# A Fourier-filter and squared-ReLU block on one core: reordered GpSimd queue, inverse stages by row group, stage-2 runs of four, and a first chunk normalised in the drain

## The chip, the cores and the metric

One core of a Trainium2 chip runs the kernel. The metric is the device time of one launch in microseconds (us). Before the change three runs gave 183.88, 184.01 and 184.28 us; the median is 184.01. The profile is of one execution, and the span of its instructions is 182.5 us.

## The reference, cut to what matters

The input is one sequence of 2048 rows of 512 bf16 values. Two residual blocks follow each other. The first normalises each row and filters it in the two-dimensional Fourier domain; the second normalises again and runs a dense layer pair with a squared ReLU.

```python
def _layernorm(x, axis=-1, eps=1e-5):
    m = jnp.mean(x, axis=axis, keepdims=True)
    v = jnp.var(x, axis=axis, keepdims=True)
    return (x - m) / jnp.sqrt(v + eps)

def _A_ref(x, w_r, w_i):                      # w_r, w_i: [2048, 257]
    X = rfft2(x.astype(float32))              # over both axes
    return irfft2(X * (w_r + 1j * w_i), s=(S, D)).astype(bfloat16)

def _B_ref(x, w1, b1, w2, b2):                # w1: [512, 1792], w2: [1792, 512]
    h = x @ w1 + b1
    r = where(h > 0, h, 0)
    return (r * r) @ w2 + b2

h  = A_x + _A_ref(_layernorm(A_x), A_w_r, A_w_i)
h2 = h   + _B_ref(_layernorm(h), B_w1, B_b1, B_w2, B_b2)
```

## The kernel before

Row number 16·p + g of the input lies in partition p, row group g (16 groups of 128 rows). Both transforms are done by matmuls with sine and cosine tables that the kernel makes itself: stage 1 (`s1`) contracts over p, stage 2 (`s2`) over the 512 columns, stage 3 (`s3`) over what is left of the rows; then comes the product with W on VectorE; stage 4 (`s4`), stage 5 (`d5` or `s5`) and stage 6 (`d6` or `s6`) go back. The rows then go through the two dense layers in five chunks of 2, 3, 4, 4 and 3 row groups (`CHUNKS`). Every task is given to a planner with an estimated duration; the planner fixes the order of each engine's instructions, and each engine keeps that order.

The normalisation of the first block is folded into the stage-1 table: `KR` is the table times the reciprocal root of a row's variance, and GpSimd computes that root. The same GpSimd queue halves one column of W (the last one) once W has been loaded.

```python
BATCH = ((0, 4), (4, 8), (8, 12), (12, 14), (14, 16))
for bi, (a, b) in enumerate(BATCH):
    ...
    pool(..., lambda a=a, b=b: gp.tensor_tensor(rs1[:, a:b], rs1[:, a:b], mhalf[:, 0:b - a], ALU.pow), z - 1,
         reads=[("va", bi), "mhalf"], writes=[("rs", bi)])                        # the roots
    for g in range(a, b):
        dve(0.22, lambda g=g: ve.tensor_scalar(flat(KR[:, g]), flat(KF[:]), rs1[:, g:g + 1], WSC, ALU.mult, ALU.mult), ...,
            reads=[("rs", bi), "KF"], writes=[("KR", g)], shared=True)
...
for k, (a, b) in (("n", (0, 9)), ("r", (9, 16))):
    for i in range(2):
        pool(0.15, lambda ...: gp.tensor_scalar(W[i][:, a:b, L - 1:L], W[i][:, a:b, L - 1:L], 0.5, None, ALU.mult), 300.0,
             reads=[("W" + k, i)], writes=[("Wh" + k, i)])                        # half of the last column
```

Stages 2 and 3 run in eight steps `pr`. The stage-2 result leaves PSUM for a bf16 tile U in which the two parts `e` of the result alternate element by element, and stage 3 reads U in straight runs. Steps 4 to 7 (`BY_PE`) take their last butterfly on TensorE (twelve matmuls), the others on VectorE (four matmuls and two additions, `bf`).

```python
def eu(...):
    U = buf(fwd, ("U", pr), "U", [P, 2, 512], BF16, 3)
    eng(U[:].rearrange("p q (c e) -> p q e c", e=2)[:, a:b], pu[:].rearrange("p (q e c) -> p q e c", e=2, c=256))
def s3(pr=pr):
    ...
    mm(a, lhsT=C, rhs=U[:, 0, :], start=True, stop=False)
    mm(b, lhsT=C, rhs=U[:, 1, :], start=True, stop=False)
    mm(a, lhsT=N, rhs=U[:, 1, :], start=False, stop=True)
    mm(b, lhsT=S_, rhs=U[:, 0, :], start=False, stop=True)
```

The stage-4 result of each step is copied to T2, whose dimensions are [quarter l, group g, q, s]. For the last step (7) four copies are made: groups 0 and 1 of each half of the quarters, then groups 2 to 15 of each half.

```python
T2 = persist.tile([P, 4, G, 16, 8], BF16, name="T2")
def et(eng=sc.copy, pr=pr, h=0, n=4, a=0, b=G):
    dst = T2[:, 2 * h:2 * h + n, :, 2 * pr:2 * pr + 2, :].rearrange("p l g q s -> p l q g s")
    ...
    eng(dst[:, :, :, a:b], src[:, 2 * h:2 * h + n, :, a:b])
```

Groups 0 and 1 (chunk 0) are not normalised before the first dense layer. A transposed copy `yt` of x minus its mean plus the filter's result is accumulated on TensorE (the x part early, in `yt_pre`, with the mean as a two-row matmul), copied to `UT0`, and multiplied by W1 as it is. Since ReLU of a positive multiple is that multiple of the ReLU, the standard deviation is put on the bias instead: each of the 14 first-layer results gets a further matmul with two contraction rows, b1 times the standard deviation, and the output is divided by the variance at the end.

```python
for f in range(NF):                                       # NF = 14
    def up(...):
        for d in range(ND):
            mm(p[:, 0:P * n], lhsT=W1[:, d, bass.ts(f, P)], rhs=(T["UT", c] if c else UT0)[:, d, 0:P * n],
               start=(d == 0), stop=(d == ND - 1 and c > 0))
    if c == 0:
        add("PE", 0.216 * n, up, reads=[("UT", c), ("FW", 0)], writes=[("pa", f)], ...)
        add("PE", 0.11, lambda f=f: mm(T["ph", 0, f][:, 0:256], lhsT=b1row[:, bass.ts(f, P)], rhs=flat(srow[:]),
                                       start=False, stop=True),
            reads=["srow", ("FW", 4)], ...)
```

Of the kernel before, what the change touches and what calls it, by code (L numbers as in the profile page):

```python
# [9 lines left out]
ALU = mybir.AluOpType  # L10
# [139 lines left out]
def kernel(  # L150
# [37 lines left out]
    T2 = persist.tile([P, 4, G, 16, 8], BF16, name="T2")  # L188
# [7 lines left out]
    sd0 = persist.tile([P, 2], FP32, name="sd0")  # L196
    mhl = persist.tile([P, 2, 2], BF16, name="mhl")
    shl = persist.tile([P, 2, 2], BF16, name="shl")
    mrow = persist.tile([2, 2, P], BF16, name="mrow")
    srow = persist.tile([2, 2, P], BF16, name="srow")  # L200
    b1row = persist.tile([2, F], BF16, name="b1row")
    one2 = persist.tile([2, P], BF16, name="one2")
# [3 lines left out]
    UT0 = persist.tile([P, ND, 2 * P], BF16, name="UT0")  # L206
# [10 lines left out]
    CN = fwd.tile([P, 4, P], BF16, name="CN")  # L217
# [29 lines left out]
    plan = Plan({"mm": 2, "sg": 4, "U": 3, "AB": 3, "X": 2, "mA": 2, "mB": 2, "Z": 2, "M": 2, "st": 4, "EO": 2,  # L247
# [33 lines left out]
    for c, (a, b) in enumerate(CH):  # L281
# [7 lines left out]
    add("SP", 0.5, lambda: sy.dma_start(b1row[:], B_b1.unsqueeze(0).to_broadcast([2, F])), writes=[("FW", 4)], prio=35,  # L289
        order=[("Wr", 1)], lag=6.0)  # L290
    for i in range(2):
        add("SP", 1.6, lambda i=i: sy.dma_start(wx[i][:].rearrange("k j l -> j k l"),
                                                wv[i].rearrange("k j l -> j k l")[9:16, ::-1, 1:L + 1]),
            writes=[("wx", i)], prio=6 + i, at=1.0, lag=6.0)
        add("SP", 1.2, lambda i=i: sy.dma_start(W[i][:, 0:9, :], wv[i][:, 0:9, 1:L + 1]), writes=[("Wn", i)],  # L295
            prio=20 + i, at=1.0, lag=7.0)
        add("SP", 0.8, lambda i=i: sy.dma_start(W[i][:, 9:16, :], wx[i][:]), reads=[("wx", i)], writes=[("Wr", i)],
            prio=22 + i, lag=5.0)
# [86 lines left out]
    for bi, (a, b) in enumerate(BATCH):  # L385
# [22 lines left out]
        for g in range(a, b):  # L408
            dve(0.22, lambda g=g: ve.tensor_scalar(flat(KR[:, g]), flat(KF[:]), rs1[:, g:g + 1], WSC, ALU.mult, ALU.mult), z - 5,  # L409
                reads=[("rs", bi), "KF"], writes=[("KR", g)], shared=True)  # L410
    for g in range(G):
# [15 lines left out]
        def e1(eng, g0, key=key):  # L427
            n = 2 if g0 < 10 else 1
            dst = Bt[:].rearrange("p e q (g s) -> p e g q s", s=8)[:, :, g0:g0 + n]
            COPY[eng](dst, T[key][:].rearrange("p (i e q s) -> p e i q s", e=4, q=16, s=8))  # L430
        if not big:
            add(("ACT", "DVE"), (0.59, 0.67), lambda e, g=g, e1=e1: e1(e, g), reads=[key], writes=["Bt"], prio=56 + g)
        elif g % 2:
            act(0.93, lambda g=g, e1=e1: e1("ACT", g - 1), 10 + g, reads=[key], writes=["Bt"])
# [12 lines left out]
    PE0, PE1, PES = 4, 8, 1  # L447
# [4 lines left out]
    for lt in range(4):  # L452
# [7 lines left out]
    dve(0.1, lambda: ve.memset(one2[:], 1.0), 190.0, writes=["one2"])  # L460
    dve(0.13, lambda: ve.tensor_copy(mhl[:, :, 0], nm1[:, 0:2]), 200.0, reads=["nm1"], writes=["mh"], shared=True)
    dve(0.13, lambda: ve.tensor_tensor(mhl[:, :, 1], nm1[:, 0:2], mhl[:, :, 0], ALU.subtract), 200.0, reads=["mh"],
        writes=["mhl"], shared=True)

    dve(0.15, lambda: ve.tensor_copy(b1f[:], b1b[:]), 200.0, reads=[("FW", 2)], writes=["b1f"], shared=True)

    def mid_tasks():
        act(1.07, lambda: sin_of(flat(GI[:]), lo(flat(fiI[:]))), 125.0, reads=["fiI"], writes=["GI"])
        act(1.4, lambda: sc.activation(junk[:, 0:1], eps[:], ACT.Sqrt), 0.0, reads=["GI", "eps", ("p4", SQ)], writes=["sqrt"])
        def mr():  # L470
            p = sg_tile(("mr", 0))
            for g in range(2):
                mm(p[0:2, P * g:P * g + P], lhsT=mhl[:, g, :], rhs=ident[:], start=True, stop=True)
        add("PE", 0.12, mr, reads=["mhl", "ident"], writes=[("mr", 0)], prio=110.0, alloc=("sg", ("mr", 0)))
        act(0.25, lambda: sc.copy(flat(mrow[:]), T["mr", 0][0:2, 0:2 * P]), 110.0, reads=[("mr", 0)], writes=["mrow"])

        def yt_pre(g):
            y = sg_tile(("yt", g))
            mm(y[:], lhsT=one2[:], rhs=mrow[:, g].unsqueeze(1).to_broadcast([2, 4, P]), start=True, stop=False)
            for d in range(ND):  # L480
                mm(y[:, P * d:P * d + P], lhsT=xs[:, g, P * d:P * d + P], rhs=ident[:], start=False, stop=False)
        for g in range(2):
            add("PE", 0.44, lambda g=g: yt_pre(g), reads=["mrow", "one2", "ident"], writes=[("yt", g, 0)], prio=145.0 + g,
                uses=[("yt", g)], alloc=("sg", ("yt", g)))

    for k, (a, b) in (("n", (0, 9)), ("r", (9, 16))):
        for i in range(2):
            pool(0.15, lambda i=i, a=a, b=b: gp.tensor_scalar(W[i][:, a:b, L - 1:L], W[i][:, a:b, L - 1:L], 0.5, None,
                                                              ALU.mult), 300.0,
                 reads=[("W" + k, i)], writes=[("Wh" + k, i)])  # L490
    gfv = GF[:].rearrange("p t r (e j) -> p t r e j", e=2)
    Z0 = 80

    for pr, first in ((0, 1), (1, 1), *((p, 0) for p in range(8))):
# [12 lines left out]
        if first or pr > 1:  # L507
# [12 lines left out]
            def eu(pr=pr, a=0, b=2, eng=sc.copy, new=True):  # L520
                U = buf(fwd, ("U", pr), "U", [P, 2, 512], BF16, 3) if new else T["U", pr]
                pu = T[("p2", pr, a) if pr < 2 else ("p2", pr)]
                eng(U[:].rearrange("p q (c e) -> p q e c", e=2)[:, a:b], pu[:].rearrange("p (q e c) -> p q e c", e=2, c=256))
            if pr < 2:
                for q in range(2):
                    add(("ACT", "DVE"), (0.66, 0.7), lambda e, pr=pr, eu=eu, q=q: eu(pr, q, q + 1, COPY[e], q == 0),
                        reads=[("p2", pr, q)], order=[("U", pr, 0)] * q, writes=[("U", pr), ("U", pr, q)],
                        alloc=None if q else ("U", ("U", pr)), prio=z + 2)
            else:
                act(1.17, eu, z + 2, reads=[("p2", pr)], writes=[("U", pr)], alloc=("U", ("U", pr)))  # L530

        ab = ("X", pr) if pr == 0 or pr in BY_PE else ("AB", pr)
        if pr == 0 and first:
            def s3z(u):
# [3 lines left out]
                mm(o[:], lhsT=C, rhs=U[:, u, :], start=True, stop=False)  # L538
                mm(o[:, 0:256], lhsT=S_, rhs=U[:, u, 256:512], start=False, stop=False)
                mm(o[:, 256:512], lhsT=N, rhs=U[:, u, 0:256], start=False, stop=True)  # L540

            def ea0(u, eng):
                X = buf(fwd, ("X", 0), "AB", [P, 2, 2, 256], BF16, 3) if u == 0 else T["X", 0]
                eng(flat(X[:, u]), T["p3", 0, u][:])
            for u in range(2):
                add("PE", 0.46, lambda u=u, s3z=s3z: s3z(u), reads=[("U", 0, u), "EF0", "EF1", "EF2"], order=[("p3", 0, j) for j in range(u)],
                    writes=[("p3", 0, u)], prio=z + 1, alloc=("sg", ("p3", 0, u)))
                add(("ACT", "DVE"), (0.59, 0.67), lambda e, u=u, ea0=ea0: ea0(u, COPY[e]), prio=z + 1, reads=[("p3", 0, u)],
                    order=[("X", 0, 0)] * u, writes=[("X", 0), ("X", 0, u)], alloc=None if u else ("AB", ("X", 0)))
        elif pr > 0 and not first:  # L550
            def s3(pr=pr):
# [4 lines left out]
                if pr in BY_PE:  # L556
                    Cn = CN[:, BY_PE.index(pr), :]
                    r, i = slice(0, 256), slice(256, 512)
                    mm(a, lhsT=C, rhs=U[:, 0, :], start=True, stop=False)
                    mm(b, lhsT=C, rhs=U[:, 0, :], start=True, stop=False)  # L560
                    mm(a[:, r], lhsT=C, rhs=U[:, 1, i], start=False, stop=False)
                    mm(b[:, i], lhsT=C, rhs=U[:, 1, r], start=False, stop=False)
                    mm(a[:, i], lhsT=Cn, rhs=U[:, 1, r], start=False, stop=False)
                    mm(b[:, r], lhsT=Cn, rhs=U[:, 1, i], start=False, stop=False)
                    mm(a[:, r], lhsT=S_, rhs=U[:, 0, i], start=False, stop=False)
                    mm(b[:, i], lhsT=S_, rhs=U[:, 0, r], start=False, stop=False)
                    mm(a[:, i], lhsT=N, rhs=U[:, 0, r], start=False, stop=False)
                    mm(b[:, r], lhsT=N, rhs=U[:, 0, i], start=False, stop=False)
                    mm(a, lhsT=N, rhs=U[:, 1, :], start=False, stop=True)
                    mm(b, lhsT=N, rhs=U[:, 1, :], start=False, stop=True)  # L570
                else:
                    mm(a, lhsT=C, rhs=U[:, 0, :], start=True, stop=False)
                    mm(b, lhsT=C, rhs=U[:, 1, :], start=True, stop=False)
                    mm(a, lhsT=N, rhs=U[:, 1, :], start=False, stop=True)
                    mm(b, lhsT=S_, rhs=U[:, 0, :], start=False, stop=True)
# [23 lines left out]
        def prod(pr=pr, i=0):  # L599
            m = buf(fwd, (("mA", "mB")[i], pr), ("mA", "mB")[i], [P, 2, 2, 256], BF16, 2)  # L600
            sel = slice(0, 9, 8) if pr == 0 else slice(pr, 17 - pr, 16 - 2 * pr)
            ve.tensor_tensor(m[:], T["X", pr][:], W[i][:, sel].unsqueeze(2).to_broadcast([P, 2, 2, 256]), ALU.mult)
        for i in range(2):
# [46 lines left out]
        def et(eng=sc.copy, pr=pr, h=0, n=4, a=0, b=G):  # L650
            dst = T2[:, 2 * h:2 * h + n, :, 2 * pr:2 * pr + 2, :].rearrange("p l g q s -> p l q g s")
            src = T["p4", pr][:].rearrange("p (l q g s) -> p l q g s", l=4, q=2, g=G)
            eng(dst[:, :, :, a:b], src[:, 2 * h:2 * h + n, :, a:b])  # L653
        if pr < 7:
            act(0.93, et, z + 3, reads=[("p4", pr)], writes=["T2", "T2a"])
        else:
            for h in range(2):
                add(("ACT", "DVE"), (0.25, 0.22), lambda e, h=h, et=et: et(COPY[e], 7, h, 2, 0, 2), prio=z, reads=[("p4", 7)],
                    writes=["T2a", ("T2a", h)])
                add(("ACT", "DVE"), (0.53, 0.6), lambda e, h=h, et=et: et(COPY[e], 7, h, 2, 2, 16), prio=z + 90,  # L660
                    reads=[("p4", 7)], order=["T2a"], writes=["T2", ("T2r", h)])

# [29 lines left out]
    for g in range(2):  # L692
        for e in (1, 0):
            ptag = "pp" if g else "po"

            def d5(g=g, e=e, ptag=ptag):
                p = bank(("pd", g, e), ptag, 3 if g else 2)
                for r in range(2):
                    mm(p[:, 0:256], lhsT=flat(T2[:, 2 * r + e, g]), rhs=GI[:, 2 * r + e, :], start=(r == 0), stop=(r == 1))
# [7 lines left out]

            def yt(g=g, e=e):
# [251 lines left out]
```

## Time and profile before

| what | value |
|---|---|
| median time | 184.01 us (183.88 to 184.28) |
| span of the profiled execution | 182.5 us |
| PE, matmul, busy | 164.4 us (90%), 1096 instructions |
| DVE busy | 123.6 us (68%) |
| ACT busy | 110.3 us (60%) |
| POOL busy | 15.3 us (8%) |
| chain that ended last | PE 75%, DVE 9%, DMA 7% |

PE is TensorE, DVE VectorE, ACT ScalarE, POOL GpSimd, and SPq the queue that issues the transfers. The profile's line of 40 slices gives the busy tenths of each engine in slices of 4.6 us. The chain of work that ended last starts at the last instruction and goes back, at each step, to what released it. Its pieces are printed in order of time as start, duration and what ran. A timeline row has the start, the duration and the instruction with its count; square brackets give the idle time of the engine before it and what ended it. [...] a group of matmuls is better measured from the start of one to the start of the next.

### The profile page before, as it was taken

The page shows a single profiled execution, that of the slowest core. Times are in us where ns is not written, and L with a number is a line of the kernel's source. Part 1 is how long each engine was busy: PE and PEld are TensorE (multiplying, and loading weights), DVE is VectorE, ACT ScalarE, POOL GpSimd, SP SyncE. Part 2 cuts the span into 40 slices and gives each one's busy share as a digit, 9 for nine tenths or more (in the row PEclk, how much of TensorE's full clock was granted, in tenths as well). Part 3 has the DMA queues.
Part 4 walks back from the last instruction along what each step waited for, and adds up shares of the span by engine and source line. Part 5 has one row for each costly group of instructions (what it writes and reads, how often), then busy time and mean ns, then how long its engine had stood idle before and what let it go on. Part 6 is the DMA issues. An engine that isn't in the chain of part 4 may idle for free.

```text
span 182.5 us, 2994 instructions
## 1 busy us (share of the span) xinstructions
PE 164.4 (90%) x1096; PEld 97.7 (54%) x1112; DVE 123.6 (68%) x350; ACT 110.3 (60%) x206; POOL 15.3 (8%) x38
## 2 busy tenths in 40 slices
PE   7976429899999499999999999999999999999992
PEld 4466317576776376555755555444554445455440
DVE  4996125886989469653899739998639995257311
ACT  3996403798979377652789718882528973058300
POOL 8842035000000000000000000000000000000000
PEclk9999966999999999999999999999999999999999
DMA  5959999970000000000100010000110000100010
GB/s 147 311 129 161 222 297 278 387 241 0 0 2 4 0 0 4 0 2 29 32 0 0 29 44 17 0 2 29 36 56 0 0 0 32 56 31 0 0 57 29
DMA packets 15599, 12.15 MB, mean 67 GB/s; under 512 B 6112, under 2 KB 14176, under 8 KB 15586
## 3 DMA queue, kind: packets, MB, share of 16 engines
q1 hardware_dynamic: 15586, 11.97, 23.7%
q8 instruction: 8, 0.13, 0.3%
q14 instruction: 5, 0.04, 0.1%
HBM read 8.92 MB, written 3.01 MB: 65 GB/s over the span
## 4 chain that ended last, share of the span: by engine, by line
PE 75%; DVE 9%; DMA 7%; SPq 2%; issue 2%; ACT 2%; POOL 1%; POOLq 0%; DVEq 0%; ACTq 0%
PE po L913 26%; PE sg L885 18%; PE ph L885 9%; DMA xs<-in_A_x_dram 4%; DMA W<-wx 4%; PE m_p L513 3%; DVE st L398 2%; PE pp L862 2%; DVE KR L409 2%; PE m_p L643 1%; SPq L295 1%; PE pp L764 1%; DVE Z L610 1%; PE pp L757 1%; PE s_p L513 1%
## 5 line engine op out<-in xcount | busy, mean ns | idle before, releaser
L913 PE MATMUL po<-W,act 128*128 128x512 bf16 x215 | 49.9, 379 | 0.4
L885 PE MATMUL sg<-UT,W 128*128 128x512 bf16 (+2 forms) x182 | 37.7, 337 | 0.1
L885 PEld LDWEIGHTS <-W 128*128 128x128 bf16 x280 | 25.9, 98 | 20.6 <-issue 0.3
L898 ACT ACTIVATE rl<-sg,b1f 128x512 bf16<-128x512 f32 (+1 forms) x37 | 23.2, 634 | 18.8 <-PE sg L885 17.4
L913 PEld LDWEIGHTS <-act 128*128 128x128 bf16 x224 | 21.4, 98 | 24.0
L904 DVE TENSOR_TENSOR act<-rl 128x384 bf16<-128x384 bf16 (+2 forms) x70 | 24.9, 367 | 9.6 <-ACT rl L898 9.1
L924 DVE TENSOR_TENSOR ot<-po,hb 128x512 bf16<-128x512 f32 x14 | 9.7, 691 | 19.3 <-PE po L913 19.2
L885 PE MATMUL ph<-UT,W 128*128 128x384 bf16 (+2 forms) x96 | 20.4, 335 | 0.3 <-ACT UT L717 0.2
L898 ACT ACTIVATE rl<-ph,b1f 128x384 bf16<-128x384 f32 (+1 forms) x19 | 12.0, 630 | 4.3 <-PE ph L885 3.6
L664 ACT ACTIVATE junk<-hs,nm 128x512 bf16<-128x512 bf16 x14 | 10.0, 714 | 3.8 <-DVE hs L785 3.8
L788 DVE TENSOR_TENSOR hb<-hs,b2b 128x512 f32<-128x512 bf16 x16 | 10.7, 681 | 0.0
L785 DVE TENSOR_TENSOR hs<-pp,xs 128x512 bf16<-128x512 f32 x14 | 9.6, 689 | 1.2 <-PE pp L757 0.7
L420 PE MATMUL s_p<-KR,xs 128*128 128x256 bf16 x12 | 4.3, 364 | 6.1 <-DVE KR L409 6.0
L253 PEld LDWEIGHTS <-fz 128*128 128x128 bf16 x104 | 7.5, 109 | 4.2 <-issue 2.2
L653 ACT CAST T<-m_p 128x1024 bf16<-128x1024 f32 (+2 forms) x9 | 7.6, 871 | 2.5 <-DVE T L653 2.5
L409 DVE TENSOR_SCALAR KR<-KF,rs 128x256 bf16<-128x256 bf16 x16 | 4.0, 307 | 7.2 <-POOL rs L405 7.2
L582 ACT CAST AB<-m_p 128x1024 bf16<-128x1024 f32 x7 | 7.0, 1007 | 2.7 <-ACT T L653 1.0
L643 PE MATMUL m_p<-EI,M 128*128 128x256 bf16 x56 | 7.6, 274 | 0.7 <-DVE M L621 0.5
L780 DVE TENSOR_TENSOR R<-q 128x127 bf16<-128x127 f32 x36 | 8.3, 284 | 0.0
L398 DVE BATCH_NORM_STATS2 st<-xs 128x6 f32<-128x512 bf16 x12 | 7.7, 673 | 0.3 <-DMA xs<-in_A_x_dram 0.3
L849 ACT ACTIVATE u<-hs,nr,rs 128x512 bf16<-128x512 bf16 x7 | 5.6, 810 | 3.7 <-DVE nr L841 3.7
L422 PEld LDWEIGHTS <-xs 128*128 128x128 bf16 x32 | 3.5, 108 | 7.9 <-issue 7.3
(204 smaller groups left out, 268.3 us busy)
## 6 DMA issues: line engine op xcount, KB each, us to landing
W<-in_B_w_dram SPq DMA_DIRECT2D x2, 1792.0 KB, 10.1
out_dram<-ot SPq DMA_DIRECT2D x16, 128.0 KB, 1.8
xs<-in_A_x_dram SPq DMA_DIRECT2D x3, 512.0 KB, 6.7
W<-wx SPq DMA_DIRECT2D x2, 448.0 KB, 6.7
W<-in_A_w_r_dram SPq DMA_DIRECT2D x1, 576.0 KB, 5.4
W<-in_A_w_i_dram SPq DMA_DIRECT2D x1, 576.0 KB, 7.5
xs<-in_A_x_dram SPq DMA_DIRECT2D x2, 256.0 KB, 3.8
wx<-in_A_w_r_dram SPq DMA_DIRECT2D x1, 448.0 KB
```

Of the source, the lines that this page charges most:

```text
L398: ve.bn_stats(st[:], xs[:, g, :])
L409: dve(0.22, lambda g=g: ve.tensor_scalar(flat(KR[:, g]), flat(KF[:]), rs1[:, g:g + 1], WSC, ALU.mult, ALU.mult), z - 5, reads=[("rs", bi), ...
L643: mm(o, lhsT=mv[:, u, r, e, :], rhs=EI[:, 1 - u:3 - u, pr, :], start=(u == 0), stop=(u == 1))
L664: sc.activation(junk[:], src, ACT.Square, bias=nm1[:, g:g + 1], accum_out=ss2[:, g:g + 1])
L780: ve.tensor_tensor(o, x, y, (ALU.add, ALU.subtract, ALU.subtract, ALU.add)[k])
L785: dve(0.66, lambda g=g: ve.tensor_tensor(hs[:, g, :], T["p6", g][:], xs[:, g, :], ALU.add), z, reads=[("p6", g)], writes=[("hs", g)])
L788: dve(0.62, lambda g=g: ve.tensor_tensor(hb[:, g, :], hs[:, g, :], b2b[:], ALU.add), late + 180 + g, reads=[("hs", g), ("FW", 3)], order=[ ...
L885: mm(p[:, 0:P * n], lhsT=W1[:, d, bass.ts(f, P)], rhs=(T["UT", c] if c else UT0)[:, d, 0:P * n], start=(d == 0), stop=(d == ND - 1 and c > 0))
L898: sc.activation(r[:, 0:P * n], T["ph", c, f][:, 0:P * n], ACT.Relu, bias=b1f[:, f:f + 1] if c else 0.0, scale=1.0)
L904: ve.tensor_tensor(t[:, f, 0:P * n], r[:, 0:P * n], r[:, 0:P * n], ALU.mult)
L913: mm(p[:], lhsT=T["act", c][:, f, bass.ts(i, P)], rhs=W2[:, f, :], start=(f == 0), stop=(f == NF - 1))
L924: ve.tensor_tensor(o[:], T["po", g][:], hb[:, g, :], ALU.add)
```

## The change

It has four parts, and some moves that go with them.

- **W column.** The halving of W's column now also reads the last batch of roots (`("rs", 4)`), so it stands behind all roots in GpSimd's queue.
- **Stage 2.** U is written in runs of four elements of each part instead of element by element, and stage 3 reads it through a stepped pattern. The first step's evictions are split over ScalarE and VectorE, as are those of stage 1's last groups (10 to 15), and the first step's products are split in two. One step (4) goes from `BY_PE` to the VectorE butterfly. U has two buffers instead of three.
- **T2.** The row group becomes the outermost dimension of T2. The last step's copies are by groups: 0 to 1, 2 to 7, 8 to 15; stage 5 of a group below 8 needs only the first two.
- **Chunk 0.** `yt`, the two-row matmuls, the rows of means and deviations and the final division go. Groups 0 and 1 are normalised like all others, straight from the PSUM tile of stage 6, transposed on TensorE and copied. The transposed tiles of all chunks get a layout by group, so that their copies are contiguous.

```diff
-                 reads=[("W" + k, i)], writes=[("Wh" + k, i)])
+                 reads=[("W" + k, i), ("rs", 4)], writes=[("Wh" + k, i)])
-    PE0, PE1, PES = 4, 8, 1
+    PE0, PE1, PES = 5, 8, 1
+    RUN = 4
+    def mu(o, w, U, q, s, **k):
+        mm(o.rearrange("p (j i e) -> p j i e", e=2, i=RUN), lhsT=w,
+           rhs=U[:, q, s].rearrange("p (j e i) -> p j i e", e=2, i=RUN), **k)
-                eng(U[:].rearrange("p q (c e) -> p q e c", e=2)[:, a:b], pu[:].rearrange("p (q e c) -> p q e c", e=2, c=256))
+                eng(U[:].rearrange("p q (j e i) -> p q e j i", e=2, i=RUN)[:, a:b],
+                    pu[:].rearrange("p (q e j i) -> p q e j i", e=2, i=RUN, q=b - a))
...
-                    mm(a, lhsT=C, rhs=U[:, 0, :], start=True, stop=False)
+                    mu(a, C, U, 0, slice(None), start=True, stop=False)
...
-    T2 = persist.tile([P, 4, G, 16, 8], BF16, name="T2")
+    T2 = persist.tile([P, G, 4, 16, 8], BF16, name="T2")
...
-            for h in range(2):
-                add(("ACT", "DVE"), (0.25, 0.22), lambda e, h=h, et=et: et(COPY[e], 7, h, 2, 0, 2), ..., writes=["T2a", ("T2a", h)])
-                add(("ACT", "DVE"), (0.53, 0.6), lambda e, h=h, et=et: et(COPY[e], 7, h, 2, 2, 16), ..., writes=["T2", ("T2r", h)])
+            add(("ACT", "DVE"), (0.28, 0.28), lambda e, et=et: et(COPY[e], 7, 0, 2), ..., writes=["T2a"])
+            add(("ACT", "DVE"), (0.5, 0.53), lambda e, et=et: et(COPY[e], 7, 2, 8), ..., order=["T2a"], writes=["T2b"])
+            add(("ACT", "DVE"), (0.58, 0.62), lambda e, et=et: et(COPY[e], 7, 8, G), ..., order=["T2a"], writes=["T2"])
...
+                def un0(g=g):
+                    u = buf(ffn, ("u", 0), "u2", [P, 4, D], BF16, 2) if g == 0 else T["u", 0]
+                    if g:
+                        ve.tensor_scalar(u[:, 1, :], T["py", 1][:], nm1[:, 1:2], rs2[:, 1:2], ALU.add, ALU.mult)
+                    else:
+                        sc.activation(u[:, 0, :], T["py", 0][:], ACT.Identity, scale=rs2[:, 0:1], bias=nr2[:, 0:1])
+                def tr0(g=g):
+                    p = bank(("pt", 0, g), "po", 2, BF16)
+                    for d in range(ND):
+                        pe.transpose(p[:, P * d:P * d + P], T["u", 0][:, g, bass.ts(d, P)], ident[:])
...
-            if c == 0:
-                add("PE", 0.216 * n, up, reads=[("UT", c), ("FW", 0)], writes=[("pa", f)], ...)
-                add("PE", 0.11, lambda f=f: mm(T["ph", 0, f][:, 0:256], lhsT=b1row[:, bass.ts(f, P)], rhs=flat(srow[:]), ...
-            else:
+            add("PE", 0.216 * n, up, reads=[("UT", c), ("FW", 0)], writes=[("ph", c, f)], prio=z, alloc=(tag, ("ph", c, f)))
```

## The prediction, made before the changed kernel had run

> **What bounds the kernel now.** I read the busy tenths of the profile's page first, then the chain of waits in order of time, then timelines of single engines where the chain leaves PE.
>
> ```profile
> PE   7976429899999499999999999999999999999992
> ...
> PEclk9999966999999999999999999999999999999999
> ```
>
> One slice is 4.6 us. PE is nearly full from 27 us on, except for one slice near 61 us. Between 18 and 27 us it has a hole (digits 4 and 2), and its granted clock falls to 0.6 in the slice in which the hole ends. The chain says what fills the hole:
>
> ```profile
> 19.13 6.74 DMA W<-wx
> 25.95 0.38 POOL W L488
> 26.33 0.77 issue
> 27.10 0.30 POOLq L955
> 27.40 0.68 POOL rs L405
> 28.11 0.54 DVE KR L409
> ```
>
> A load of W, then the halving of its column, then a root, then the stage-1 table made from that root. The root has no use for W. GpSimd's own timeline shows that it only stands behind it in the queue:
>
> ```profile
> 22.10 0.29 POOL L488 TENSOR_SCALAR W<-W 128x9 bf16<-128x9 bf16 x1 [6.89 <-DMA W<-in_A_w_r_dram]
> 24.81 0.28 POOL L488 TENSOR_SCALAR W<-W 128x9 bf16<-128x9 bf16 x1 [2.42 <-DMA W<-in_A_w_i_dram]
> 25.02 0.73 POOL L405 TENSOR_TENSOR rs<-rs,mhalf 128x2 f32<-128x2 f32 x1
> ```
>
> GpSimd sat idle 6.89 and 2.42 us for the loads, while the input of that root (VectorE, L403, 16.36 to 16.52 in the timeline) was ready 8.5 us earlier. Stage 1 so ends at 30.3, and stage 2 starts at 31.23.
>
> From 31.23 to 61.84 (the end of stage 4) VectorE carries the chain more than PE: in the windows 43 to 47 and 47 to 51 it is busy 3.97 and 4.00 of 4 us. Then comes the drain:
>
> ```profile
> 61.84 0.23 DVE L653 CAST T<-m_p 128x64 bf16<-128x64 f32 x1 [1.03 <-PE m_p L643]
> 62.10 0.21 ACT L653 CAST T<-m_p 128x64 bf16<-128x64 f32 x1 [1.84 <-DVE T L653]
> ...
> 62.35 0.62 DVE L653 CAST T<-m_p 128x448 bf16<-128x448 f32 x1 [0.28 <-ACT T L653]
> 63.01 0.53 ACT L653 CAST T<-m_p 128x448 bf16<-128x448 f32 x1 [0.69 <-DVE T L653]
> 63.59 0.60 PE L699 MATMUL po<-GI,T 128*128 128x256 bf16 x4 [1.78 <-ACT T L653]
> ```
>
> The four copies to T2 run one after the other on two engines, and stage 5 of groups 0 and 1, which needs the two small ones, waits for all of them: 1.78 us of idle PE. First-layer matmuls start at 67.47. In chunk 0 each of the 14 results costs:
>
> ```profile
> 71.52 0.61 PE L885 MATMUL sg<-UT,W 128*128 128x256 bf16 x4
> 72.06 0.28 PE L889 MATMUL sg<-srow,b1row 2*128 2x256 bf16 x1
> 72.27 0.61 PE L885 MATMUL sg<-UT,W 128*128 128x256 bf16 x4
> ```
>
> 0.75 us from start to start. Four matmuls of 256 columns take 0.44 (67.47 to 67.91 in the same timeline), so the two-row bias matmul costs 0.31, not the 0.11 its columns would take. Chunk 1 starts at 86.39, and from there to 182.5 PE alone is the bound, in the same instruction order before and after.
>
> [...] Stage 3's new pattern reads eight bf16 elements[...] in the order 0, 4, 1, 5 and so on. [...] the trace has no stepped moving operand of any length, only reversed ones, at full rate (L764: 8 matmuls of 127 columns in 0.45 us). [...] the two KR instructions at 28.11 took 0.98 us beside GpSimd's fiI work, 0.48 at 25.78. [...]
>
> **The change part by part.**
>
> 1. W column. The root of groups 12 to 13 can start at about 16.6 and end at 17.3. The last pair's has another brake: in VectorE's new order its input stands behind a copy of group 10's stage-1 result, which PE has ready at 18.84. So copy (0.42, as L704's of 256 elements) to 19.26, input (0.17) to 19.43, root (0.73) to 20.25. PE finishes groups 8 to 11 at 20.1, then does 12 and 13 (0.44 each) to 21.0. The last two tables follow copies on VectorE, at 21.2 to 21.7; groups 14 and 15 end at 22.45, their copies, split over two engines, at 23.1. **Stage 2 starts at about 23.3 instead of 31.23: −7.9.** [...]
>
> 2. Does W come in time? Its four halvings can end near 22.3, 25.0, 26.2 and 27.4 (landings from the same timeline plus 0.3). From stage 2's start to the first product took 3.44 us before (34.67 − 31.23). With every eviction split (two of 0.4 rather than one of 0.7 at each of two steps) I expect 2.3, so the first product is at 25.5. W's real part is there; the imaginary one by 25.0 too. The transposed tables that stage 4 reads land at 29.07 before, and a dropped 0.3 us issue helps; stage 4's first step wants them at about 28.8. All three meet, but none is late by more than half a microsecond. First product **−9.2** in all.
>
> 3. The middle. Before, the first product to the end of stage 4 took 27.2 us (34.67 to 61.84). VectorE's work is 8 steps of two products, two Z and (but one) two M, at 0.61, 0.34 and 0.34, about 20 us; three butterflies add 2.0. The new one adds 0.7; PE loses eight matmuls, 0.86 us (its steps 4 to 7 take 1.73 each, the others 0.87). ScalarE's six large U copies cost 1.18 apiece from start to start (3.67 for three), and those written in runs of 8 or more 0.95; at that rate −1.4. `yt_pre` and `mr` leave PE (two of 0.66, and 0.2). Following the new orders with these durations, ScalarE feeds the last step at 45.5, VectorE ends it at 49.5, and stage 4 ends at 50.7. I add 0.8 for GpSimd's fiI and W work (3.1 us) that now lies beside VectorE's products: **end of stage 4 at 51.5 instead of 61.84, −10.3.**
>
> 4. Drain and chunk 0. Let E be that end. Before: first-layer start E+5.63, chunk 1 at E+24.55. After: one T2 copy of 0.3, stage 5 at E+0.35 (before E+1.75); stage 6 of group 1 done at E+2.55. Then a chain that was not there: statistics (0.9 on ScalarE, 0.86 on VectorE), root, reciprocal and scale, each shared with work of group 2, to E+4.6; normalisation 0.7; transposes; copy. By the new orders group 1 normalises at E+5.9 to 6.6, and its copy ends at E+7.7: **the first layer starts 2.1 later, at E+7.8.** But PE does stage 5 and two stage 6 of chunk 1 meanwhile. What remains is 14 × 0.44 = 6.1, 28 second-layer matmuls × 0.216 = 6.05, one stage 6 (0.45) and twelve transposes (0.66): 13.3. **Chunk 1 at E+21.1 instead of E+24.55: −3.4.** The removed bias matmuls alone are 14 × 0.31 = 4.3.
>
> Sum: −10.3 − 3.4 = −13.7, or 170.3. Chains worked out by hand leave out small waits, so I put it at **171.3 us**.
>
> **The rivals.** (a) The stepped read halves stage 3's rate. Stage 3 has 22,528 columns[...]. PE's middle would be 23.5 + 9.4 = 33 us from 23.3, and PE would become the bound: E near 57, time near 177. For it: no such read in the trace. [...] (b) W or the tables become the bound once roots don't wait: the page's DMA row shows nine tenths or more in each slice from 14 to 37 us, and a landing 2 us later than before would pass straight into the time: 173 to 174. (c) The new chain in the drain is longer: nine steps over two engines, a tenth or two more on each gives 1 to 2 us, 172 to 173. (d) VectorE is the bound of the middle, so the moved butterfly costs its 0.7 and U's cheaper copy gives nothing, if ScalarE was waiting anyway: 172. (e) All waits of the middle stay as they were (27.2), only the start moves: E at 52.7, 172.5.
>
> **Range and chances.** (b) to (e) together are worth up to +3, (a) alone +6 at perhaps one in eight. Below, a middle without the 0.8 and a better drain give −2.5. So 168.6 to 176.0. Even (a) with (c) stays under 180.3, so faster by over 2% has 0.95.
>
> **What would show it.** Right: GpSimd's roots all before its first W row; stage 2's first matmul near 23; stage 3's groups of four still 0.87 apart; first product near 25.5; stage 4's end near 51.5; stage 5 under 0.6 us after it; first-layer start 7 to 9 us after it, then 0.44 per result. Wrong: stage 3's matmuls at over 0.3 us apart; VectorE idle for a DMA after 25; a PE hole of over 8 us in the drain.

## The result, and the profile after

The changed kernel takes **175.43 us** (175.0 to 176.3 in four runs) against 184.14 for the kernel before; the ratio is 0.953, with a 95% interval of 0.949 to 0.958. The forecast had 171.3 us with a range of 168.6 to 176.0. So the time lies in the range, but of 12.7 us that were forecast only 8.7 came. The profile says where the rest stayed, and the experiments say why. The profiled execution is the one of 176.32 us; its span is 174.5.

The first view is the page's busy tenths of 40 slices, here of 4.4 us each.

```profile
PE   7955978999976779999999999999999999999991
...
PEclk9999999999998769999999999999999999999999
```

The hole with the empty slice before 27 us has gone, and with it the half clock there (0.50 from 23.76 to 30.59 us in the trace of before). But there is a new soft place, at the 12th to 15th slice (48 to 65 us): the drain between stage 4 and the first layer. Its clock falls, too (8, 7 and 6 tenths), which it did not do in the profile before. GpSimd's timeline shows the part of the change that worked as meant:

```profile
16.76 0.70 POOL L395 TENSOR_TENSOR rs<-rs,mhalf 128x2 f32<-128x2 f32 x1 [1.39 <-DVE mv L390]
19.68 0.70 POOL L395 TENSOR_TENSOR rs<-rs,mhalf 128x2 f32<-128x2 f32 x1 [2.22 <-DVE rs L393]
21.96 0.30 POOL L462 TENSOR_SCALAR W<-W 128x9 bf16<-128x9 bf16 x1 [1.58 <-DMA W<-in_A_w_r_dram]
```

The last two roots run before the first halving of W's column, the last of them at 19.68 where it was 27.34 before. Now the two places that are late. The first is the way from stage 2 to the first product, from ScalarE's and VectorE's timelines (start, duration, instruction, then in brackets the idle time before it and what ended it):

```profile
24.42 0.37 ACT L507 CAST U<-s_p 128x256 bf16<-128x256 f32 x1 [0.70 <-PE s_p L491]
25.61 0.37 ACT L507 CAST U<-s_p 128x256 bf16<-128x256 f32 x1 [0.82 <-DVE U L507]
...
24.82 0.76 DVE L507 CAST U<-s_p 128x256 bf16<-128x256 f32 x2 [1.43 <-ACT U L507]
27.41 0.67 DVE L600 TENSOR_TENSOR mA<-AB,W 128x512 bf16<-128x512 bf16 x1
```

The two halves of a stage-2 result, which lie in one PSUM tile, were to be copied by two engines at once. They go one after the other: ScalarE, VectorE twice, ScalarE, and each waits for the other engine's copy. The second place is the drain, where the T2 copies do the same. Stage 5 (`po`) of groups 0 and 1 reads only what the first of them wrote, by 53.62, but it starts after the last, which ends at 54.85:

```profile
53.33 0.29 DVE L656 CAST T<-m_p 128x128 bf16<-128x128 f32 x1 [1.03 <-PE m_p L646]
53.65 0.48 ACT L656 CAST T<-m_p 128x384 bf16<-128x384 f32 x1 [0.85 <-DVE T L656]
54.16 0.69 DVE L656 CAST T<-m_p 128x512 bf16<-128x512 f32 x1 [0.55 <-ACT T L656]
54.91 0.61 PE L703 MATMUL po<-GI,T 128*128 128x256 bf16 x4 [1.62 <-DVE T L656]
```

The stretches of the same trace, cut where the granted clock changes (stretch, its length, busy time and instructions of PE, weight loads, VectorE, ScalarE and GpSimd, then the clock, the DMA share and its GB/s):

```profile
51.94:55.35 3.41, 1.70 (x14) 1.19 (x14) 1.34 (x4) 1.37 (x3) 0.00 (x0) 1.00 0.00 0
55.35:58.77 3.42, 3.42 (x15) 1.82 (x13) 0.85 (x2) 1.49 (x4) 0.00 (x0) 0.50 0.00 0
58.77:62.18 3.41, 1.63 (x26) 1.36 (x24) 2.88 (x11) 2.32 (x7) 0.00 (x0) 1.00 0.00 0
62.18:65.59 3.41, 2.88 (x24) 2.26 (x22) 2.93 (x8) 2.53 (x7) 0.00 (x0) 0.50 0.00 0
```

Two stretches of 3.41 us in which PE was busy for 1.70 and 1.63 us are each followed by one at half clock. Stages 5 and 6 of chunk 0 and the start of the first layer fall into the two at half clock. Each of the four executions of the changed kernel lost at least one such stretch: their mean clocks are 0.98, 0.99, 0.98 and 0.99, and one stretch at half clock takes 0.01 off the mean (half of 3.41 us in a span of 174.5). The old drain was no safer: a stretch of 3.41 us laid from 60.0 in the trace of before has PE busy for 1.28 us, and with the old drain the executions of w_gi and old_chunk0 profiled below lost their clock in it (0.50 from 55.06 to 58.48 and from 54.85 to 58.26 us).

The milestones, in us of the trace (E, the end of stage 4, is read as the start of its last step's first T2 copy; the last three rows give the time since the milestone above):

| | before | forecast | after |
|---|---|---|---|
| stage 2 starts | 31.23 | 23.3 | 23.77 |
| first product | 34.67 | 25.5 | 27.41 |
| E | 61.84 | 51.5 | 53.33 |
| stage 5, from E | 1.75 | 0.35 | 1.58 |
| first layer, from stage 5 | 3.88 | 7.45 | 9.41 |
| chunk 1, from first layer | 18.76 | 13.3 | 13.91 |

From the start of chunk 1 to the end both kernels take 96.3 us. Up to E the change brought 8.5 us where 10.3 were forecast; between E and chunk 1 it brought nothing (24.4 before, 24.9 after) where 3.3 were forecast from these readings.

### The profile page after: what moved, and what is told of

The parts are those of the page before. It is cut to its first block, busy times and chain, and to the rows that moved or that the text cites. A ratio compares the mean times of both kernels' runs of the same rounds, so it can differ in the third digit from the quotient of the medians.

```text
span 174.5 us, 2942 instructions
## 1 busy us (share of the span) xinstructions
PE 158.3 (91%) x1072; PEld 95.1 (54%) x1072; DVE 123.8 (71%) x356; ACT 110.3 (63%) x210; POOL 15.6 (9%) x38
## 4 chain that ended last, share of the span: by engine, by line
PE 79%; ACT 7%; DVE 6%; DMA 3%; issue 2%; SPq 0%; DVEq 0%; ACTq 0%
PE po L908 28%; PE sg L887 18%; PE ph L887 10%; PE m_p L470 5%; DMA xs<-in_A_x_dram 3%; PE m_p L491 3%; PE pp L865 2%; PE m_p L646 2%; PE pp L755 2%; ACT junk L379 1%; PE pp L748 1%; ACT junk L382 1%; ACT Bt L420 1%; DVE Bt L420 1%; PE m_p L245 1%
## 5 line engine op out<-in xcount | busy, mean ns | idle before, releaser
L908 PE MATMUL po<-W,act 128*128 128x512 bf16 x224 | 50.6, 379 | 0.0
L893 ACT ACTIVATE rl<-sg,b1f 128x512 bf16<-128x512 f32 (+2 forms) x46 | 27.4, 603 | 17.6 <-PE sg L887 16.1
L887 PEld LDWEIGHTS <-W 128*128 128x128 bf16 x280 | 27.0, 99 | 19.3
L899 DVE TENSOR_TENSOR act<-rl 128x384 bf16<-128x384 bf16 (+2 forms) x70 | 24.9, 368 | 7.3 <-ACT rl L893 6.1
L916 DVE TENSOR_TENSOR ot<-po,hb 128x512 bf16<-128x512 f32 x16 | 11.1, 691 | 21.5 <-PE po L908 21.4
L893 ACT ACTIVATE rl<-ph,b1f 128x384 bf16<-128x384 f32 (+2 forms) x24 | 14.3, 597 | 5.0 <-PE ph L887 4.4
L470 PE MATMUL m_p<-U,EF 128*128 128x512 bf16 (+1 forms) x46 | 9.4, 337 | 0.1
L656 ACT CAST T<-m_p 128x1024 bf16<-128x1024 f32 (+1 forms) x8 | 7.7, 962 | 2.0 <-PE m_p L646 1.2
L245 PEld LDWEIGHTS <-fz 128*128 128x128 bf16 x100 | 6.7, 104 | 3.9 <-issue 2.3
L491 PEld LDWEIGHTS <-Bt 128*128 128x128 bf16 x64 | 6.1, 98 | 2.9 <-ACT Bt L420 1.0
L646 PEld LDWEIGHTS <-M 128*128 128x128 bf16 x56 | 5.1, 98 | 3.9 <-DVE M L624 1.8
```

Of the source, the lines that this page charges most:

```text
L245: mm(p[:, 0:P], lhsT=fz[:, 0:P], rhs=fz[:, 0:P], start=True, stop=True)
L470: mm(o.rearrange("p (j i e) -> p j i e", e=2, i=RUN), lhsT=w, rhs=U[:, q, s].rearrange("p (j e i) -> p j i e", e=2, i=RUN), **k)
L491: mm(puv[:, e, :], lhsT=Bt[:, 2 * t + 1 - e, 2 * pr + q, :], rhs=gfv[:, t, :, e, :], start=(t == 0), stop=(t == 1))
L646: mm(o, lhsT=mv[:, u, r, e, :], rhs=EI[:, 1 - u:3 - u, pr, :], start=(u == 0), stop=(u == 1))
L887: mm(p[:, 0:P * n], lhsT=W1[:, d, bass.ts(f, P)], rhs=T["UT", c][:, 0:n, d, :], start=(d == 0), stop=(d == ND - 1))
L893: sc.activation(r[:, 0:P * n], T["ph", c, f][:, 0:P * n], ACT.Relu, bias=b1f[:, f:f + 1], scale=1.0)
```

## The experiments

**The W column alone (w_order), then with the sine (w_gi).** The edit, in the kernel before:

```diff
-                 reads=[("W" + k, i)], writes=[("Wh" + k, i)])
+                 reads=[("W" + k, i), ("rs", 4)], writes=[("Wh" + k, i)])
```

> The kernel before, with one change alone: the halvings of W's column wait behind the last root. Theory (the start of stage 2 carries over whole, stage 2 near 23.3 instead of 31.23 us): 184.1 - 7.9 = 176.2 us, so nearly all of the 8.7 us that the whole change brought. Rival (the loads of W or of the transposed tables take the place of the wait): a VectorE wait for a DMA in the first product or a PE wait for the tables, and 177.5 to 179 us. Rival (the other parts are worth 3 us or more, as the forecast had it): 179 us would be needed for that sum, too.

Measured: 180.25 us (178.76 to 181.25), ratio 0.978 (0.972 to 0.985). None of the three expectations fits. Stage 2 starts at 24.34 (stage 1 ran at half clock from 15.89 to 19.30 in the profiled execution) and the first product is at 27.84, still 6.8 us earlier than before; but from there to E it takes 28.44 us instead of 27.17. ScalarE's timeline shows a wait that is new:

```profile
29.71 1.06 ACT L270 ACTIVATE GI<-fiI 128x1024 bf16<-128x1024 int16 x1 [1.97 <-POOL fiI L453]
```

The sine table of the inverse stages stands in ScalarE's queue for angles (fiI) which stand in GpSimd's queue behind the four halvings. The whole change moved this table as well, to a place behind step 4, which my forecast did not list as a part. So I moved it:

```diff
-        act(1.07, lambda: sin_of(flat(GI[:]), lo(flat(fiI[:]))), 125.0, reads=["fiI"], writes=["GI"])
+        act(1.07, lambda: sin_of(flat(GI[:]), lo(flat(fiI[:]))), 142.0, reads=["fiI"], order=[("p3", 4)], writes=["GI"])
```

> The kernel before with the halvings behind the last root, as w_order, and with the sine table of the last stage at its new place in ScalarE's order, behind stage 3's result of step 4. Theory (in w_order the sine stands in ScalarE's queue for GpSimd's angles, which stand behind the halvings, and the evictions wait 2 us with it): the stretch from the first product to the end of stage 4 is 27 us or less instead of 28.4, and the time is 178.6 us where w_order has 180.25, or 177.2 against 178.8 where the clock holds in stage 1. Rival (the stretch is long for another reason): 28.4 us again, 180 us.

Measured: 177.49 us (175.76 to 179.11), ratio 0.960 (0.953 to 0.968), and 27.09 us from the first product to E. The reordering of two queues is thus worth about 7 us; taken alone, the first half of it gave 4. The sine's wait is 1.4 us of the 2.8 between the two medians (28.44 against 27.09 us in the middle, and 178.76 against 177.45 us for the profiled executions). The rest lies within the scatter of each kernel, 2.5 and 3.4 us.

**The old chunk 0 (old_chunk0).** The drain and chunk 0 as in the kernel before, everything ahead of them as in the changed one (the diff is the change's chunk-0 and T2 parts, reversed).

> The changed kernel with chunk 0 and the drain by the old route (bias row, 1/scale at the output, the old T2 order), everything ahead of the drain changed. Theory (the new chunk 0 as it ran gave back all that the bias matmuls cost): end of stage 4 at 53.3, chunk 1 at E + 24.6 as before, 175.5 us, the same as the changed kernel within 0.7. Rival (the forecast's -3.4 was there and the middle lost it): 178.8 us.

Measured: 176.26 us (175.38 to 177.0), ratio 0.957 (0.951 to 0.963), against 0.953 (0.949 to 0.958) of the changed kernel. The new chunk 0 as it ran was worth 0.8 us, and the intervals overlap. The theory, the same within 0.7, missed by 0.1; the rival, 178.8, fell. Both kernels lost clock in the drain in their profiled executions, from E to chunk 1 26.05 us here and 24.90 there.

**Keeping PE at work in the drain (warm).** Fifteen matmuls of zeros whose results nothing reads:

```diff
+                if g == 0 and e == 1:
+                    keep(6, "sg")          # ahead of stage 5: six matmuls of 512 columns
                 p = bank(("pd", g, e), ptag, 3 if g else 2)
...
+                    if g == 4:
+                        keep(5, "ph")      # behind stage 5 of group 4
...
+                    keep(2, "ph")          # ahead of each transposition of chunk 0
```

> The changed kernel with 15 extra matmuls of 512 zeros, whose results nothing reads: six while stage 5 waits for the T2 copies, five behind stage 5 of group 4, two ahead of each transposition of chunk 0. Theory (the half clock from 55.35 to 58.77 and from 62.18 to 65.59 follows the PE gaps of the drain and costs 1.7 and some 0.7 us on its path): no step of the clock in the drain, chunk 1 at E + 22.6, and 173.0 us, with less scatter from run to run. Rival (the chain over ScalarE and VectorE sets the start of the first layer, whatever the clock): 175.2 us. Rival (the fillers stand in PE's way): 176 us.

Measured: **173.32 us** in all four runs (173.32 to 173.33), ratio 0.941 (0.937 to 0.945). The same kind of stretches as above:

```profile
51.94:55.35 3.41, 3.04 (x21) 2.04 (x23) 1.26 (x3) 1.31 (x4) 0.00 (x0) 1.00 0.00 0
55.35:58.77 3.42, 3.21 (x28) 1.88 (x26) 2.40 (x10) 2.13 (x8) 0.00 (x0) 1.00 0.00 0
```

The clock stays at 1.00, and chunk 1 starts at E + 22.38 instead of E + 24.90. More work on PE made the kernel 2.1 us faster. That the four runs agree within 0.01 us was luck in part: in stage 1 a stretch laid from 11.75 has PE busy for only 1.03 us, and base2 below, with the same fifteen matmuls, lost its clock there. The chain over ScalarE and VectorE was not what was late: from stage 5 to the first layer it now takes 7.50 us (forecast 7.45), and chunk 0 from there 13.30 (forecast 13.3). Set against the old chunk 0 in the executions whose mean clock was 1.00 (175.38 and 175.57 us), the new one is worth 2.1 us once the clock holds, against 3.3 forecast.

**Whole evictions (whole_evict).** The splits in stage 1, stage 2 and stage 3 of step 0 undone, one engine for one tile:

```diff
-                    for h in range(2):     # U 0, half h: ScalarE, VectorE
-                        add(("ACT", "DVE")[h], (0.42, 0.45)[h], lambda q=q, h=h, eu0=eu0: eu0(q, h), ...
+                    add(("ACT", "DVE"), (0.6, 0.67), lambda e, ...: eu(pr, q, q + 1, COPY[e], q == 0), ...
```

> The changed kernel with the evictions of stage 1's last groups, of U 0 and of stage 3's step 0 whole again, one engine for one bank. Theory ([...] a split buys nothing): first product 3.4 to 3.7 us after stage 2's start and 175.4 us, within 0.4. Rival (each split saved 0.3 us as forecast, and something else is late): 176.0 to 176.6 us.

Measured: 171.82 us (171.66 to 174.35), ratio 0.933 (0.928 to 0.937). I had expected no difference; both theories missed by 3.6 us or more. Evictions of stage 2, then of stage 3's step 0, in the timelines of VectorE and ScalarE:

```profile
23.33 0.69 DVE L501 CAST U<-s_p 128x512 bf16<-128x512 f32 x1 [1.03 <-PE s_p L491]
24.20 0.69 DVE L501 CAST U<-s_p 128x512 bf16<-128x512 f32 x1 [0.18 <-PE s_p L491]
...
23.77 0.59 ACT L501 CAST U<-s_p 128x512 bf16<-128x512 f32 x1 [1.14 <-PE s_p L491]
...
25.07 0.69 DVE L523 CAST AB<-s_p 128x512 bf16<-128x512 f32 x1 [0.18 <-PE s_p L470]
25.51 0.59 ACT L523 CAST AB<-s_p 128x512 bf16<-128x512 f32 x1 [0.28 <-PE s_p L470]
```

Copies of different PSUM tiles overlap (VectorE to 24.02, ScalarE from 23.77), and each waits for PE alone. A shared destination does not prevent it: the two copies of stage 3's step 0 (L523) write one SBUF tile and overlap as well (25.07 to 25.76 and 25.51 to 26.10). So what made the halves take turns in these runs was the shared source. Against the run with extra matmuls, whose clock held too, stage 2 starts 0.6 us earlier (22.68 against 23.31), the first product comes after 3.18 instead of 3.64, and the middle takes 25.41 instead of 25.91: together 1.6 us, the difference of 173.32 and 171.7. The other 2 us are the drain's clock, which held in three of the four executions (mean clock 1.00; the fourth, at 174.35 us, has 0.98). In the profiled one it held by where its stretches fell: 1.74 us busy between 51.16 and 54.57, while one laid from 55.75 would have had 1.13. So the splits did not merely earn nothing; the three together cost 1.6 us.

**Both together (base2).**

> The changed kernel with whole evictions and with the 15 extra matmuls of zeros in the drain: both edits that helped, together. Theory (they are independent: one moves the start of the middle, the other keeps the clock): 171.7 us as the best runs of whole evictions alone, but in every run, with a scatter under 0.1. Rival (the whole evictions were faster only because the clock happened to hold): 173.3 us, as the extra matmuls alone.

Measured: 171.88 us median, 171.7 in the best two of five and 173.66 in the profiled one. The rival fell, but the scatter stayed: the profiled execution lost its clock in another place, stage 1, after a stretch with 1.36 us of PE:

```profile
12.26:15.67 3.41, 1.36 (x17) 1.10 (x15) 3.41 (x12) 3.41 (x6) 1.96 (x2) 1.00 1.02 168
15.67:19.09 3.42, 3.42 (x29) 2.99 (x27) 1.17 (x8) 0.51 (x1) 0.70 (x1) 0.50 0.78 164
```

**Stage 4's last result in two tiles (t2_two).** On the kernel of base2; ScalarE copies one tile to T2, VectorE the other. Four extra matmuls instead of six stand ahead of stage 5.

```diff
-            pt = mm_tile(("p4", pr)) if half == 0 else T["p4", pr]      # one tile of 1024 columns
+            if pr == 7: pt = sg_tile(("p4", 7, half))                   # two tiles of 512 columns
...
+                add(("ACT", "DVE")[h], 0.23, ... eth(h, 0, 2), reads=[("p4", 7, h)], writes=["T2a"])
+                add(("ACT", "DVE")[h], (0.53, 0.6)[h], ... eth(h, 2, G), reads=[("p4", 7, h)], writes=["T2b", "T2"])
```

> As the kernel of base2, but the last result of stage 4 lies in two tiles of one PSUM bank each from the pool that stays open, and ScalarE copies one half to T2 and VectorE the other. Theory (copies of one tile by two engines wait for each other, and stage 5's result waits for the last of them because it takes over the tile's place): the copies run side by side, stage 5 starts 0.4 us after the end of stage 4 instead of 1.58, and the time falls by 1.1 to 170.6 us. Rival (the chain over the statistics sets the first layer whatever stage 5 does, or the place is not the cause): stage 5 at E + 1.5 or the first layer no earlier, 171.7 us.

Measured: 171.76 us median of four with 170.73 in the profiled run, whose clock held, and 171.2 to 172.5 in the others. ScalarE's, VectorE's and PE's timelines:

```profile
50.75 0.65 ACT L652 CAST T<-s_p 128x64 bf16<-128x64 f32 x2 [0.86 <-PE s_p L635]
...
51.19 0.76 DVE L652 CAST T<-s_p 128x64 bf16<-128x64 f32 x2 [1.03 <-PE s_p L635]
...
51.85 0.60 PE L701 MATMUL po<-GI,T 128*128 128x256 bf16 x4
```

The copies overlap, and stage 5 follows E (here the start of VectorE's copy, 51.19) after 0.66 us instead of 1.58. Where the clock held that is 1.0 us (170.73 against 171.7): the theory, with 1.1 expected. Stage 5 starts at 51.85, before VectorE's second copy ends at 51.95, so it no longer waits for the last copy. In the kernels without this edit its result goes to a place in PSUM that the source of T2 held before, in a pool opened when that one is released; the new tiles lie in a pool that stays open. The run changes the tiles and their place at once, so it does not part the two causes. PE now comes to stage 5 straight from the extra matmuls, which may hold it for part of the 0.66.

**The chain first (norm_first).** On base2: VectorE's steps of chunk 1 come behind chunk 0's normalisation.

```diff
-                        order=[("qh", g)] * i,
+                        order=[("qh", g)] * i + [("un", 1)] * (c == 1),
```

> As the kernel of base2, but the VectorE steps of chunk 1's stage 5 come behind the normalisation of chunk 0 instead of between its steps. Theory (the ninefold chain to the first layer is lengthened by work of groups 2 to 4 that stands between): first layer some 1.5 us earlier, half of it given back where chunk 1's work falls beside the first layer's results, so 170.7 us. Rival (ScalarE, full with the relus of the first layer, pays all of it back): 171.7 us; (chunk 1's transposes come late) 172.5 us.

Measured: 172.65 us (171.77 to 173.47), no faster than base2. In the profiled execution the first layer starts 6.29 us after stage 5 instead of 7.49, and chunk 0 takes 14.62 from there instead of 13.30. PE's timeline shows what came back:

```profile
59.06 0.60 PE L883 MATMUL ph<-UT,W 128*128 128x256 bf16 x4 [0.67 <-ACT UT L829]
59.50 0.61 PE L750 MATMUL pp<-qb,KI 128*128 128x127 bf16 x8
...
59.97 0.61 PE L750 MATMUL pp<-qb,KI 128*128 128x127 bf16 x8
```

Two stage 6 of chunk 1 (0.47 and 0.48 to what follows), which in base2 ran in PE's waits ahead of the first result, now stand behind it. The wait was shortened by the very work that had been done in it.

**Runs of one (runs1).** On base2, `RUN = 4` becomes `RUN = 1`.

> As the kernel of base2, with stage 2's results again interleaved element by element (runs of one instead of four). Theory (VectorE is full in the middle, ScalarE's cheaper copies are hidden): each U copy 1.31 us instead of 1.0, the stretch from the first product to the end of stage 4 longer by 0 to 0.5, 171.7 to 172.2 us. Rival (ScalarE feeds that stretch, as the forecast's -1.4 had it): 173.1 us.

Measured: 172.68 us (172.66 to 174.34). The groups of ScalarE's instructions give the U copies, in runs of one, then (from base2) in runs of four:

```profile
L501 ACT CAST U<-m_p 128x1024 bf16<-128x1024 f32 x6 | 8.0, 1366 | 0.2 <-ACT T L642 0.2
```

```profile
L501 ACT CAST U<-m_p 128x1024 bf16<-128x1024 f32 x6 | 6.3, 1063 | 0.2 <-ACT T L642 0.2
```

0.30 us less for each of six copies; the middle is 26.34 us long with runs of one, 25.26 with runs of four. The part is worth 1.0 us, between the two expectations (172.2 and 173.1): although VectorE is busy 15.5 of the 16 us from 31 to 47 in this run (15.8 in base2), more than half of ScalarE's 1.8 us shows.

**All that helped, and stage 1 filled (best1).** On the kernel with two tiles: five more matmuls of zeros ahead of group 0, six ahead of group 4.

```diff
+            if g in (0, 4):
+                p = psg.tile([P, 512], FP32, tag="sg", name="s_w", bufs=nps[1])
+                for _ in range((5, 6)[g // 4]):
+                    mm(p[:], lhsT=fz[:, 0:P], rhs=fz[:], start=True, stop=True)
```

> As the kernel of t2_two, with eleven more matmuls of zeros in stage 1: five ahead of group 0 and six ahead of group 4, where PE stands idle for tables and evictions. Theory (a stretch of 3.41 us in which PE is busy for less than about half is followed by one at half clock, and stage 1's hole from 13.3 to 14.9 us is the last such stretch): no step of the clock at all, every run within 0.2 of 170.7 us. Rival (the scatter of 170.7 to 172.5 has another cause, such as the loads): the scatter stays, median 171.7 us. Rival (the fillers stand in stage 1's way): stage 2 later than 22.7 and 171 us or more.

Measured: **170.8 us** (170.72 to 170.92 in six runs), ratio 0.927 (0.923 to 0.932). It is faster than both kernels, and its scatter is 0.2 us where the kernel with two tiles had 1.8. The page's clock line:

```profile
PEclk9999999999999999999999999999999999999999
```

## Why the prediction was right or wrong

1. **W column: right.** Forecast 23.3 for stage 2, 23.77 measured, 23.31 in two other runs with the same instructions up to there, 22.68 without the splits. So the forecast met its number with a split that cost 0.6 us. No table or load took the wait's place (rival b): w_gi has the first product at 26.18 with the old evictions. What the step left out is that the halvings delay GpSimd's angles; without the sine's new place that costs 1.4 us of the middle. Nor did the clock hold in stage 1 in every execution: those profiled of w_order and base2 ran it at 0.50 from 15.89 to 19.30 and from 15.67 to 19.09 us.
2. **First product: wrong.** "With every eviction split (two of 0.4 rather than one of 0.7 at each of two steps) I expect 2.3." It was 3.64, and 3.18 with no split at all. Halves of one tile ran in turn: in the trace of after no two copies of one tile overlap among those of U (24.42 to 25.98 us), of step 0 (ScalarE to 26.30 and 27.04, VectorE from 26.34 and 27.07) and of T2 (53.33 to 54.85). The profile puts the wait of each later copy down to the other engine's; the runs do not show what would happen if the copies met.
3. **Middle: right, in part by luck.** Forecast 26.0 from first product to E, measured 25.92. Stage 3's stepped reads ran at full rate (four matmuls of 512 columns in 0.87 us, as in the kernel before), so rival (a) fell; its 9.4 us was an estimate, and 22,528 columns at that pace are 9.6. The term for U was forecast as −1.4 and is −0.9 to −1.1 (26.34 against 25.41 and 25.26). The splits cost 0.5 here that the forecast did not have (25.91 against 25.41), and the allowance of 0.8 covered both errors. The allowance, made for GpSimd's work beside the products, may show in part: of the three 512-element products that start while GpSimd works on the angles (26.41 to 28.68 us), two took 0.67 and 0.61 us; the third took 0.41, as did the one behind them. Both long ones write mA, and no run parts that from GpSimd's work, so the cause was not shown.
4. **Drain and chunk 0: wrong by 3.8 us**, in two terms of the sum. "One T2 copy of 0.3, stage 5 at E+0.35" was E+1.58, so 1.2 us late: stage 5 waited for all three copies, which took turns, and not for the one that it reads. In t2_two 0.9 of it went. My own lines of the kernel before showed both: at 62.10 a ScalarE copy from the other half of the same tile starts only when VectorE's has ended (61.84 to 62.07), and stage 5 waits for the last of four. The two copies read different columns; what they shared was the tile. I read the wait as the old order's fault. And nothing in the step allowed for the clock: 2.5 us in the profiled execution (24.90 against 22.38), 2.1 in the medians. The step also read the start of chunk 1 in the kernel before as 86.39; the trace has it at 86.23, so the forecast gain was 3.3 and not 3.4. All other terms held: the ninefold chain (7.50 against 7.45, rival c), 0.44 per result, 13.3 for chunk 0.

Put right, the sum closes. From 175.43, the clock in the drain (2.1), the splits (1.6) and the tile (1.0) leave 170.7; 170.8 is what the last kernel takes, and 170.3 was the bare sum of the forecast. So the plan of the change was sound. What it lost lay in how tiles are shared and in what PE does while it waits, and the range held the result by luck: none of the rivals (a) to (e), for which it was made that wide, is what happened.

## What to carry to other kernels

Before splitting an eviction over two engines, give each engine a tile of its own: in the changed kernel the readers of one tile took turns (T2's copies from 53.33 to 54.85 us), and stage 5 began at 54.91, behind the last one, E + 1.58; with a tile for each engine it began at E + 0.66. When work on a fuller engine is removed, look at what PE does in the waits that remain: in these traces each stretch of 3.41 us that half clock followed had PE busy for 1.70 us or less, and fifteen cheap matmuls in the drain were worth 2.1 us. When an instruction moves behind another in a queue, follow everything that reads what now comes later (here the sine table, 1.4 us).

## What the runs showed of the hardware

- **The clock falls long before PE is idle.** The longest gap of the changed kernel's drain is 1.62 us, and it lost its clock twice (0.50 from 55.35 to 58.77 and from 62.18 to 65.59 us). I cut twelve traces into stretches of 3.41 us at the phase of their clock changes: 512 stretches up to 150 us. Eight are followed by half clock, with PE busy for 0.00, 1.05, 1.06, 1.27, 1.36, 1.55, 1.63 and 1.70 us. Of the other 504 only two lie under 1.70 (1.57 and 1.62). So in these runs the line lies near half a stretch (1.71 us), and it is not sharp. Nor do the stretches begin at one time of the kernel: the first of them begins at 0.74 us in the trace of after, at 3.28 in that of before, and between 0.23 and 3.37 us in all twelve. That fits what the last kernel shows: wherever one lays a stretch of 3.41 us between 4 and 82 us (tried in steps of 0.25), PE is busy for at least 2.56 in it, and all six runs agree within 0.2 us. One profiled execution does not settle it for the others: the one of t2_two has nothing under 1.91 there, and two of the other three lost clock (0.987 and 0.990).
- **Matmuls of zeros count.** The fillers multiply zeros by zeros; with them the two stretches of the drain from 51.94 had PE busy for 3.04 and 3.21 us and kept the clock at 1.00, where without them the first had 1.70 and 0.50 followed.
- **A stepped moving operand** in runs of four bf16 elements cost nothing against straight reading (four matmuls of 512 columns in 0.87 us either way, in after and before), and the runs of four cut ScalarE's writing from 1.37 (runs1) to 1.06 us (base2) for 1024 elements.
